# Attention and gated convolution FFN on one core: scores of three pairs in other PSUM banks, one load queue, a shared buffer pool, planned constants, and new due times

## The chip, the cores and the metric

The kernel runs on one core of one Trainium2 chip. The metric is the device time of one execution in microseconds; the median of 3 runs of the kernel before is 542.69 us (542.3 to 543.33). Lower is better. The five engines are called PE (TensorE, matmul; its weight loads are shown apart as PEld), DVE (VectorE), ACT (ScalarE), POOL (GpSimd) and SP (SyncE, which here only issues transfers).

## The reference

Eight batches of 576 rows. First a masked attention with 8 heads of 64: the first four heads see the last 32 positions, the other four see 32 positions at a distance of 4. Then a feed-forward block with a convolution of three taps along the rows as its gate.

```python
scores = (q @ k.T) / 8                       # per batch and head, 576 x 576
plain   = (rel >= 0) & (rel < 32)            # heads 0..3
dilated = (rel >= 0) & (rel < 128) & (rel % 4 == 0)   # heads 4..7
attn = softmax(where(mask, scores, -1e9));  x = attn @ v     # -> (8, 576, 512)
h = relu(x @ w_in)                           # 512 -> 1024
conv = sum(conv_w[k] * h shifted by k - 1)   # 3 taps along the rows
out = (h * sigmoid(conv)) @ w_out            # 1024 -> 512
```

## The kernel before, in words

**Pairs.** Each batch has four pairs of heads (`attention(b, p)`; p 0 and 1 plain, 2 and 3 dilated). Only the band that the mask lets through is computed. Per pair: SP loads `qk` and `v`; PE computes the scores into three of the four banks of the PSUM buffer `att` (`scores`, L255); the softmax runs on DVE and ACT; DVE transposes (L298); PE multiplies with `v` into the same `att` buffer (`values`, L309); ACT copies the high part of x (L359) and DVE subtracts to get the low part (L375). There is one `att` buffer, and a pair holds it once from its scores to its exponentials and once from its values to its subtraction. The first 8 pairs (those of batches 0 and 1) are "eased": PE adds the mask into the bank by matmuls with a matrix of ones (L244), DVE takes maxima (L265, L267), and ACT does nine exponentials of 64 columns with a bias and a running sum (L275). The other 24 pairs add the mask and sum on DVE (L280 to L292).

**Products.** `expert(b, ...)` multiplies x by `w_in` (L398, 16 groups of 12 matmuls a batch: three terms, high and low parts) in the PSUM buffers `mm` (two banks; in batch 0 also `nn`), ACT takes the relu into `h` (L405), ACT and DVE form the three taps (L416, L410), the sigmoid (L421), the gate (L423) and its high and low parts in `g` (L426, L428). The second product (L440, 36 blocks of 24 matmuls) accumulates in `nn` (two banks), ACT copies it to `out` (L451) and SP stores it (L454).

**Weights.** The weights come as 64-bit numbers. `weights` loads a 512 KB tile as pairs of 32-bit words into an `out` buffer, by a transfer issued from POOL (L466), and rebuilds it: one ACT pass (L473), then DVE steps (L475, L478, L480, L483, L486). For the first nine tiles (all eight of `w_in`, one of `w_out`) PE sums the parts (L495 to L497) and ACT copies high and low (L492, L500); for the other seven DVE adds and subtracts (L502, L508).

**Constants.** At the head, outside the plan, in this order on ACT: the mask is loaded by ACT's own queue and spread into `mask_sb` (L518 to L522), after that come the matrices `minus` and `ones` (L512, L513). In the program that runs, the first weight tile's ACT pass stands between the two.

**Order.** Nothing runs in loop order. Each piece of work is a `Task` with an engine, a cost and a due time; `Planner.order` simulates the engines and writes the order out: on each engine, of the tasks that could start within 0.25 us of the earliest, the one with the smallest due time goes next. Buffers are pools of slots; a task whose slot isn't free waits in that simulation. The due times are the tables `DUE` (products, gates, second products of each batch), `PAIR`, `WI` and `WO`. The chip executes each engine's and each queue's list strictly in that order, with semaphores where data or slots demand it.

Of the kernel before, what the change touches and what calls it, by code (L numbers as in the profile page):

```python
# [8 lines left out]
F32 = mybir.dt.float32  # L9
# [25 lines left out]
    0: (580.8, 27.9, -1.4),  # L35
    1: (213.6, -299.0, 236.5),
    2: (298.7, 74.3, 336.3),
    3: (207.5, 235.5, 370.3),
    4: (392.2, 246.5, 569.0),
    5: (236.9, 118.2, 411.6),  # L40
    6: (240.1, 311.5, 692.5),
    7: (425.8, 381.5, 859.4),
}
PAIR = {
    0: (-457.5, -556.4, -489.6, -298.9),
    1: (-233.9, -88.4, -68.9, 30.4),
    2: (100.4, 158.5, 106.2, 115.4),
    3: (159.5, 176.7, 263.5, 224.6),
    4: (271.0, 337.4, 174.1, 173.0),
    5: (406.9, 395.3, 384.0, 446.3),  # L50
    6: (231.2, 489.6, 330.6, 394.1),
    7: (590.7, 577.9, 625.9, 591.3),
}
WI = (-419.2, 32.4, -71.8, -195.1, -259.0, 8.1, -51.2, -117.3)
WO = (47.2, 77.7, 55.2, 78.0, 38.6, 19.0, 87.9, 102.0)
AHEAD = (8.0, 4.1, 0.0)
ONE = dict(start=True, stop=True, skip_group_check=True)


class Buffer:  # L60


    def __init__(self, pool):
        self.pool, self.left, self.end, self.t = pool, 0, 0.0, None
# [10 lines left out]
class Planner:  # L75

    LATENCY = {"DVE": 0.05, "ACT": 0.05, "SP": 2.0, "POOL": 3.0, "E": 0.2, "S": 0.33, "T": 0.35, "V": 0.2}
    OVERLAP = {"DVE": 0.08, "ACT": 0.095}
    GAP = 0.035
    WINDOW = 0.25  # L80
# [17 lines left out]
    def start(self, t, last, mode):  # L98
        at = 0.0
        if last is not None:  # L100
            at = last.end + (0.0 if t.engine == "PE" else self.GAP if last in t.after else -self.OVERLAP.get(t.engine, 0.0))
        for p in t.after:
            if p.engine != t.engine or p.engine == "SP":
                at = max(at, p.end + self.late(p))
        for b in t.uses:
            if b.t is None:
                if not self.free[b.pool]:
                    return None
                at = max(at, min(self.free[b.pool])[0])
# [49 lines left out]
def attn_moe(ctx: ExitStack, tc: tile.TileContext, qk_p, qk_d, v_p, v_d, w_in, w_out, conv, mask, out):  # L159
# [26 lines left out]
    slots("x", 7, [128, S], F32R, 2)  # L186
# [37 lines left out]
    xs = {}  # L224

    def attention(b, p):
# [3 lines left out]
        sc, tv = Buffer("att"), Buffer("att")  # L230
        xs[b, p] = x
        eased = NP * b + p < EASED
        n = (S + KP, QD + KD)[kind]
        lq = plan.add("SP", n * 0.0017, due - AHEAD[0], lambda: nc.sync.dma_start(
            out=qk.t[:, :n], in_=(qk_p, qk_d)[kind][b, p % 2]), uses=[qk])
        lv = plan.add("SP", 1.35, due - AHEAD[1], lambda: nc.sync.dma_start(
            out=v.t, in_=(v_p, v_d)[kind][b, p % 2]), uses=[v])

        def scores():


            if eased:
                for bank, (c0, c1) in enumerate(((0, 256), (320, 576), (256, 320))):
                    nc.tensor.matmul(sc.t[:, bank, 0:c1 - c0], ones, mask_sb[:, kind, c0:c1], start=True, stop=True,  # L244
                                     skip_group_check=True)
# [3 lines left out]
            for n in order:  # L249
                for hd in range(2):  # L250
# [3 lines left out]
                    for i, (q, k) in enumerate(parts):  # L254
                        nc.tensor.matmul(sc.t[quad * 32:quad * 32 + 32, bank, c * W:c * W + W], q, k,  # L255
                                         start=i == 0 and not eased, stop=i == len(parts) - 1, skip_group_check=True)

        last = plan.add("PE", (0.8, 0.92)[kind] + (0.5 if eased else 0.0), due, scores, [lq], [qk, sc, s], "S")
# [3 lines left out]
        banks = lambda: sc.t[:, 0:2, 0:256].rearrange("p h (a k) -> p h a k", k=W)  # L262
        if eased:

            last = plan.add("DVE", 0.68, due + 1.5, lambda: nc.vector.tensor_reduce(  # L265
                out=m.t.rearrange("p (h a) -> p h a", h=2)[:, :, 0:4], in_=banks(), axis=AX.X, op=ALU.max), [last], [sc, m])
            last = plan.add("DVE", 0.215, due + 1.5, lambda: nc.vector.tensor_reduce(  # L267
                out=m.t[:, 4:5], in_=sc.t[:, 2, 0:W], axis=AX.X, op=ALU.max), [last], [sc, m])
# [3 lines left out]
            def exps():  # L272
                for i in range(9):
                    bank, c = (0, i) if i < 4 else (2, 0) if i == 4 else (1, i - 5)
                    nc.scalar.activation(out=s.t[:, i, :], in_=sc.t[:, bank, c * W:c * W + W], func=AF.Exp,  # L275
                                         scale=SCALE, bias=m.t[:, i:i + 1], accum_out=z.t[:, i:i + 1])

            last = plan.add("ACT", 2.2, due + 3.0, exps, [last], [sc, s, m, z], "exp")
        else:
            last = plan.add("DVE", 0.68, due + 1.5, lambda: nc.vector.tensor_tensor(  # L280
                out=heads(flat()), in0=banks(), in1=heads(mask_sb[:, kind]), op=ALU.add),
                [last], [sc, s])
            last = plan.add("DVE", 0.215, due + 1.5, lambda: nc.vector.tensor_tensor(
                out=s.t[:, 4], in0=sc.t[:, 2, 0:W], in1=mask_sb[:, kind, 4 * W:5 * W], op=ALU.add), [last], [sc, s])
# [16 lines left out]
        def values():  # L301
# [6 lines left out]
            def pv(quad, hd, bank, block, c0, o, n):  # L308
                nc.tensor.matmul(tv.t[hd * 64:hd * 64 + 64, bank, o:o + n],  # L309
# [52 lines left out]
        if b < HELPED:  # L362
            def less():
                main, rest = parts(x.t[0])
                for t in range(4):
                    n = 160 - t % 2 * 32 if kind == 0 else 128
# [249 lines left out]
```

## Time and profile before

| | |
|---|---|
| median of 3 runs | 542.69 us (542.3 to 543.33) |
| the profiled execution, own time | 542.24 us |
| its span, first to last instruction | 540.4 us |
| busy in the span: PE / DVE / ACT / POOL | 509.5 / 400.1 / 310.0 / 10.3 us |
| mean granted TensorE clock | 0.983 |
| HBM read, written | 41.66 MB, 9.44 MB |

The profile is of one execution. Times inside it count from the first instruction of the span. A view by stretches gives the busy time of each engine in a stretch; the chain of waits follows, from the last instruction backwards, what released each step; the groups give, for one line, engine and shape, the count, the busy time and the mean of one. Matmuls overlap each other, so that the mean of one is longer than the distance from one to the next; that distance is read from the chain, where a row with a count gives the time of so many in sequence.

### The profile page before, as it was taken

The page shows a single profiled execution, that of the slowest core. Times are in us where ns is not written, and L with a number is a line of the kernel's source. Part 1 is how long each engine was busy: PE and PEld are TensorE (multiplying, and loading weights), DVE is VectorE, ACT ScalarE, POOL GpSimd, SP SyncE. Part 2 cuts the span into 40 slices and gives each one's busy share as a digit, 9 for nine tenths or more (in the row PEclk, how much of TensorE's full clock was granted, in tenths as well). Part 3 has the DMA queues.
Part 4 walks back from the last instruction along what each step waited for, and adds up shares of the span by engine and source line. Part 5 has one row for each costly group of instructions (what it writes and reads, how often), then busy time and mean ns, then how long its engine had stood idle before and what let it go on. Part 6 is the DMA issues. An engine that isn't in the chain of part 4 may idle for free.

```text
span 540.4 us, 17510 instructions
## 1 busy us (share of the span) xinstructions
PE 509.5 (94%) x7836; PEld 442.1 (82%) x7836; DVE 400.1 (74%) x692; ACT 310.0 (57%) x662; POOL 10.3 (2%) x29
## 2 busy tenths in 40 slices
PE   1678997999999999999999999999999999999997
PEld 1446896897887799879988889879989988889985
DVE  0999999899999789986893479985869309847910
ACT  3766989653764266843773158735677318528710
POOL 1011000000000000000000000000000000000000
PEclk9889997899999999999999999999999999999999
DMA  7656533222226542152113331151102012100011
GB/s 279 222 188 244 162 119 113 90 78 84 70 78 200 187 153 101 32 149 97 52 50 99 115 117 46 32 188 54 52 30 71 21 40 70 41 22 21 0 40 58
DMA packets 17162, 52.21 MB, mean 97 GB/s; under 512 B 1968, under 2 KB 2368, under 8 KB 17088
## 3 DMA queue, kind: packets, MB, share of 16 engines
q1 hardware_dynamic: 14608, 42.61, 23.9%
q0 software_dynamic: 2336, 8.41, 4.6%
q8 instruction: 61, 1.00, 0.8%
q10 hardware_dynamic: 144, 0.08, 0.1%
q14 instruction: 13, 0.11, 0.1%
HBM read 41.66 MB, written 9.44 MB: 95 GB/s over the span
## 4 chain that ended last, share of the span: by engine, by line
PE 75%; DVE 13%; ACT 9%; DMA 1%; issue 1%; ACTq 0%; POOL 0%; POOLq 0%; DVEq 0%
PE nn L440 33%; PE mm L398 30%; PE att L309 6%; PE att L255 4%; ACT s L275 4%; DVE c L410 3%; DMA out<-in_w_in_dram 1%; DVE s L296 1%; DVE pt L298 1%; DVE c L423 1%; PE nn L495 1%; DVE m L265 1%; ACT c L421 1%; ACT c L416 1%; ACT L289 0%
## 5 line engine op out<-in xcount | busy, mean ns | idle before, releaser
L410 DVE SCALAR_TENSOR_TENSOR c<-h,conv_sb,c 128x576 f32<-128x576 f32 x128 | 103.4, 815 | 22.7 <-ACT c L416 21.0
L405 ACT ACTIVATE h<-mm 128x288 f32<-128x288 f32 x120 | 48.1, 410 | 52.3 <-PE mm L398 50.7
L451 ACT COPY out<-nn 128x512 f32<-128x512 f32 (+1 forms) x37 | 21.1, 572 | 64.5 <-PE nn L440 61.7
L309 PEld LDWEIGHTS att<-pt,v 32*64 32x64 f32 x2944 | 37.9, 135 | 17.6 <-ACT s L275 5.2
L423 DVE TENSOR_TENSOR c<-c,h 128x576 f32<-128x576 f32 x64 | 47.3, 753 | 6.2 <-ACT c L421 5.3
L416 ACT ACTIVATE c<-h,conv_sb 128x576 f32<-128x576 f32 x64 | 49.0, 777 | 1.5
L398 PE MATMUL mm<-x3a,wi 128*128 128x288 f32 x176 | 49.7, 297 | 0.0
L421 ACT ACTIVATE c<-c 128x576 f32<-128x576 f32 x64 | 42.5, 681 | 11.4 <-DVE c L410 10.7
L309 PE MATMUL att<-pt,v 32*64 32x64 f32 (+2 forms) x2944 | 41.4, 229 | 6.7 <-ACT s L275 3.4
L398 PE MATMUL mm<-x4a,wi 128*128 128x288 f32 x160 | 45.7, 300 | 0.1
L398 PE MATMUL mm<-x2a,wi 128*128 128x288 f32 x144 | 41.1, 300 | 0.0
L255 PEld LDWEIGHTS att<-qk 64*32 64x32 f32 x2432 | 29.5, 109 | 9.2 <-issue 4.0
L398 PE MATMUL mm<-x5a,wi 128*128 128x288 f32 x128 | 36.5, 300 | 0.0
L398 PE MATMUL mm<-x6a,wi 128*128 128x288 f32 x128 | 36.1, 297 | 0.0
L255 PE MATMUL att<-qk 64*32 64x64 f32 x2432 | 34.9, 232 | 0.7 <-DVE x2b L375 0.6
L398 PEld LDWEIGHTS mm<-x3a,wi 128*128 128x128 f32 x176 | 33.0, 188 | 0.4
L398 PE MATMUL mm<-x0a,wi 128*128 128x288 f32 x112 | 31.6, 298 | 0.0
L398 PE MATMUL mm<-x1a,wi 128*128 128x288 f32 x112 | 31.5, 296 | 0.0
L291 DVE TENSOR_REDUCE z<-s 128x9 f32<-128x576 f32 x24 | 17.9, 748 | 18.2 <-ACT s L289 18.1
L398 PEld LDWEIGHTS mm<-x4a,wi 128*128 128x128 f32 x160 | 30.2, 189 | 0.9 <-ACT h L405 0.5
L440 PE MATMUL nn<-wo,g5a 128*128 128x512 f32 x72 | 28.9, 402 | 0.0
L440 PE MATMUL nn<-wo,g4a 128*128 128x512 f32 x72 | 28.9, 402 | 0.0
(170 smaller groups left out, 1330.9 us busy)
## 6 DMA issues: line engine op xcount, KB each, us to landing
qk<-in_qk_d_dram SPq DMA_DIRECT2D x16, 664.0 KB, 4.0
qk<-in_qk_p_dram SPq DMA_DIRECT2D x16, 592.0 KB, 4.1
out_dram<-out SPq DMA_DIRECT2D x31, 256.0 KB, 2.0
v<-in_v_p_dram SPq DMA_DIRECT2D x16, 384.0 KB, 3.5
v<-in_v_d_dram SPq DMA_DIRECT2D x16, 384.0 KB, 3.4
out<-in_w_in_dram POOLq DMA_DIRECT2D x8, 512.0 KB, 5.0
out<-in_w_out_dram POOLq DMA_DIRECT2D x8, 512.0 KB, 3.6
out_dram<-out SPq DMA_DIRECT2D x10, 128.0 KB, 2.3
```

The lines of the kernel that those rows point to most:

```text
L255: nc.tensor.matmul(sc.t[quad * 32:quad * 32 + 32, bank, c * W:c * W + W], q, k, start=i == 0 and not eased, stop=i == len(parts) - 1, skip ...
L275: nc.scalar.activation(out=s.t[:, i, :], in_=sc.t[:, bank, c * W:c * W + W], func=AF.Exp, scale=SCALE, bias=m.t[:, i:i + 1], accum_out=z.t ...
L291: last = plan.add("DVE", 0.755, due + 3.5, lambda: nc.vector.tensor_reduce(out=nine(z.t), in_=nine(s.t), axis=AX.X, op=ALU.add), [last], [ ...
L309: nc.tensor.matmul(tv.t[hd * 64:hd * 64 + 64, bank, o:o + n], v.t[quad * 32:quad * 32 + 32, block // 2, block % 2 * 64:block % 2 * 64 + 64 ...
L398: nc.tensor.matmul(ps.t[:, 0:HALF], wi[jw][fc][:, k * 128:k * 128 + 128], x[k].t[jx][:, hf * HALF:hf * HALF + HALF], start=(k == 0 and i = ...
L405: relu.append(plan.add("ACT", 0.4, due + 1.6 * u + 1.6, lambda fc=fc, hf=hf, ps=ps: nc.scalar.activation(out=h[fc].t[:, 1 + hf * HALF:1 + ...
L410: nc.vector.scalar_tensor_tensor(out=c[fc].t, in0=h[fc].t[:, k:S + k], scalar=conv_sb[:, k, fc:fc + 1], in1=c[fc].t, op0=ALU.mult, op1=ALU ...
L416: t = plan.add("ACT", 0.777, d, lambda fc=fc: nc.scalar.activation(out=c[fc].t, in_=h[fc].t[:, 1:S + 1], func=AF.Copy, scale=conv_sb[:, 1, ...
L421: t = plan.add("ACT", 0.686, d + 1.0, lambda fc=fc: nc.scalar.activation(out=c[fc].t, in_=c[fc].t, func=AF.Sigmoid), [t], [c[fc]], "sigmoid")
L423: t = plan.add("DVE", 0.755, d + 1.5, lambda fc=fc: nc.vector.tensor_tensor(out=c[fc].t, in0=c[fc].t, in1=h[fc].t[:, 1:S + 1], op=ALU.mult ...
L440: nc.tensor.matmul(ps.t, g[k].t[jg][:, col:col + 128], wo[jw][k], start=(k == 0 and i == 0), stop=(k == NF - 1 and i == 2))
L451: t = plan.add("ACT", 0.16 + 0.00093 * (c1 - c0), out_due + 5.6 + 5.6 * u, lambda ps=ps, o=o, c0=c0, c1=c1: nc.scalar.copy(out=o.t[:, c0:c ...
```

## The change

- **Scores of pairs 2 to 4 (batch 0, p = 1, 2, 3; `EARLY`)** no longer use `att` but both `mm` banks and one `nn` bank. Batch 0's first products wait in the plan for these scores. All eight banks become one PSUM tile, `banks`, with the pools as lists of bank numbers.
- **Masks of the eased pairs** come straight from the loaded `kinds_sb`, spread by a repeating read, with 4 (plain) or 5 (dilated) matmuls instead of 3. The spreading of `mask_sb` on ACT, which the other 24 pairs need, becomes planned tasks with due time 70.
- **Constants planned.** The load of the mask goes first on SP; the identity, `ones` and `minus` are tasks with the earliest due times.
- **One queue.** The 16 weight tiles and the taps are loaded from SP instead of POOL, in one list with `qk`, `v` and the stores. They get four buffers of their own (`raw`) instead of sharing the three of `out`.
- **Shared pool.** `h`, `c` and `out` (three each) become ten `u` buffers of [128, 578]; a task that takes one for `h` must leave two free (`spare`). The taps' result now starts at word 1 of its buffer, the stored result at word 16. The two-part `w` buffers (two) become three single ones.
- **`SUMMED`**: 12 tiles instead of 9 are summed on PE: three more of `w_out`.
- **Planner**: other costs (loads, exponentials), a wait of 2.3 us behind SP tasks, first times per engine; **all due times are new**. A branch that was switched off (`HELPED = 0`) is gone.

The core of the diff:

```diff
 DUE = {
-    0: (580.8, 27.9, -1.4),
-    1: (213.6, -299.0, 236.5),
...
-    7: (425.8, 381.5, 859.4),
+    0: (57.5, 90.4, 43.3),
+    1: (-112.3, 166.0, 223.7),
...
+    4: (-0.4, 293.4, 1016.3),
...
+    7: (-57.9, 355.7, 466.1),
 PAIR = {
-    0: (-457.5, -556.4, -489.6, -298.9),
-    1: (-233.9, -88.4, -68.9, 30.4),
+    0: (-155.8, -194.5, -384.9, -185.6),
+    1: (-9.5, -339.1, -101.5, 54.3),
...
-WI = (-419.2, 32.4, -71.8, -195.1, -259.0, 8.1, -51.2, -117.3)
-WO = (47.2, 77.7, 55.2, 78.0, 38.6, 19.0, 87.9, 102.0)
+WI = (-36.6, -51.1, -44.4, -350.5, -319.7, 42.1, -78.8, -407.0)
+WO = (109.7, 15.2, 69.3, 82.8, 128.6, 116.8, 106.8, 179.0)
+MASKS = 70.0
+EASED = range(8)
+EARLY = (1, 2, 3)
+SUMMED = range(12)
+LEFT = 16
+NU, NX, NR, NW, NT = 10, 7, 4, 3, 2
...
-    LATENCY = {"DVE": 0.05, "ACT": 0.05, "SP": 2.0, "POOL": 3.0, ...
+    LATENCY = {"DVE": 0.05, "ACT": 0.05, "SP": 2.3, "POOL": 0.1, ...
+    FIRST = {"SP": 0.75, "POOL": 1.0, "PE": 4.5, "ACT": 2.5}
...
-    hs = slots("h", 3, [128, S + 2])
-    slots("c", 3, [128, S])
-    slots("out", 3, [128, 1024])
-    slots("w", 2, [128, 512], F32, 2)
+    us = slots("u", NU, [128, S + 2])
+    slots("raw", NR, [128, 1024])
+    slots("w", NW, [128, 512])
...
+    banks = psum.tile([128, 8, 512], F32, name="banks")
+    plan.pool("att", [0])
+    plan.pool("mm", [4, 5])
+    plan.pool("nn", [6, 7])
...
-        sc, tv = Buffer("att"), Buffer("att")
+        early = NP * b + p in EARLY
+        sc, tv = [Buffer(n) for n in (("mm", "mm", "nn") if early else ("att",))], Buffer("att")
...
             if eased:
-                for bank, (c0, c1) in enumerate(((0, 256), (320, 576), (256, 320))):
-                    nc.tensor.matmul(sc.t[:, bank, 0:c1 - c0], ones, mask_sb[:, kind, c0:c1], ...)
+                own = ((0, 1), (2, 3)), ((2, 4),), ((1, 1),)
+                if kind == 1:
+                    own = ((3, 1), (2, 3)), ((3, 1), (2, 3)), ((4, 1),)
+                for bank, runs in enumerate(own):
+                    c = 0
+                    for i, n in runs:
+                        nc.tensor.matmul(banks[:, at[bank], c * W:(c + n) * W]..., ones,
+                                         kinds_sb[:, i, :].unsqueeze(1).to_broadcast([128, n, W]), ...)
...
-        last = plan.add("POOL", 2.2 * f, due - AHEAD[2], lambda: nc.gpsimd.dma_start(
+        last = plan.add("SP", 0.1 + 1.4 * f, due - AHEAD[2], lambda: nc.sync.dma_start(
...
-    nc.scalar.dma_start(out=kinds_sb, in_=mask)
-    make_identity(nc, ident)
-    nc.scalar.mul(out=minus, in_=ident, mul=-1.0)
-    nc.scalar.copy(out=ones, in_=ident)
+    kinds = plan.add("SP", 0.3, -1e4, lambda: nc.sync.dma_start(out=kinds_sb, in_=mask))
+    made = plan.add("POOL", 0.6, -1e4, lambda: make_identity(nc, ident))
+    made = plan.add("ACT", 0.29, -1e4, lambda: nc.scalar.copy(out=ones, in_=ident), [made])
+    plan.add("ACT", 0.29, -1e4, lambda: nc.scalar.mul(out=minus, in_=ident, mul=-1.0), [made])
...
+        masked[kind] = plan.add("ACT", 0.72, MASKS, lambda k=kind: nc.scalar.copy(out=slot_masks[k], in_=spread(2, 10)), [kinds])
```

More of the change, by code (lines that the diff above doesn't have):

```diff
@@ L98, in start @@
     def start(self, t, last, mode):
-        at = 0.0
+        at = self.FIRST.get(t.engine, 0.0)
         if last is not None:
@@ L104, in start @@
                 at = max(at, p.end + self.late(p))
+        wanted = {}
         for b in t.uses:
             if b.t is None:
-                if not self.free[b.pool]:
-                    return None
-                at = max(at, min(self.free[b.pool])[0])
+                wanted[b.pool] = wanted.get(b.pool, b.spare) + 1
+        for pool, n in wanted.items():
+            free = self.free[pool]
+            if len(free) < n:
+                return None
+            at = max(at, min(free)[0] if n == 1 else sorted(free)[n - 1][0])
         if t.table is not None and mode is not None and t.table != mode:
@@ L361, in attention @@
             his.append(last)
[L362 to L366, printed above, removed]
-                    nc.tensor.matmul(tv.t[:, t, 0:n], minus, main[:, t] if kind else (main, rest)[t % 2][:, t // 2],
-                                     start=False, stop=True, skip_group_check=True)
-                for g in range(2 if kind == 1 else 0):
-                    nc.tensor.matmul(src(1)[:, g], minus, rest[:, g], start=False, stop=True, skip_group_check=True)
-            last = plan.add("PE", (0.42, 0.6)[kind], due + 7.2, less, his, [tv, x], "E")
-            return [plan.add("ACT", cost, due + 7.5, lambda i=i: nc.scalar.copy(out=dst(x.t[1], i), in_=val(i)),
-                             [last], [tv, x]) for i, cost in ((0, 0.6), (1, 0.21))]
         return [plan.add("DVE", cost, due + 7.5, lambda i=i: nc.vector.tensor_tensor(
@@ L491, in weights @@
             ps = Buffer("nn")
[L492 removed]
+            part = plan.add("ACT", 0.62, due, lambda: nc.scalar.copy(out=hi, in_=words(t)), [main], [t])
             def add():
[L495 to L500 removed]
+                nc.tensor.matmul(bank(ps), ident, words(t), start=True, stop=False)
+                nc.tensor.matmul(bank(ps), minus, r.t, start=False, stop=False)
+                nc.tensor.matmul(bank(ps), minus, hi, start=False, stop=True)
+            last = plan.add("PE", 1.43, due, add, [rest, part], [t, r, ps], "E")
+            return plan.add("ACT", 0.6, due, lambda: nc.scalar.copy(out=lo, in_=bank(ps)), [last], [ps])
         last = rest
[L502 to L503 removed]
+        last = step(0.53, [t, r], lambda: nc.vector.tensor_tensor(
+            out=words(t) if dst is None else dst, in0=words(t), in1=words(r), op=ALU.add))
         if dst is not None:
@@ L506, in weights @@
         hi, lo = pair
-        last = plan.add("ACT", 0.62, due, lambda: nc.scalar.copy(out=hi, in_=t()), [last], [w])
-        return step(0.53, [w], lambda: nc.vector.tensor_tensor(out=lo, in0=t(), in1=hi.bitcast(F32), op=ALU.subtract))
-    nc.scalar.dma_start(out=kinds_sb, in_=mask)
-    make_identity(nc, ident)
-    nc.scalar.mul(out=minus, in_=ident, mul=-1.0)
-    nc.scalar.copy(out=ones, in_=ident)
+        last = plan.add("ACT", 0.62, due, lambda: nc.scalar.copy(out=hi, in_=words(t)), [last], [t])
@@ L523, in attn_moe @@
-    for h, in hs:
-        nc.gpsimd.memset(h[:, 0:1], 0.0)
-        nc.gpsimd.memset(h[:, S + 1:S + 2], 0.0)
-    wired = [weights(w_in[c], 512, WI[c], pair=(wi[0][c], wi[1][c]), summed=c < SUMMED) for c in range(NF)]
+    masked = [None, None]
+    for kind, (rest, own) in enumerate(((0, lambda: nc.scalar.copy(out=slot_masks[0][:, 0:5:4, :], in_=kinds_sb[:, 0:2, :])),
+                                        (1, lambda: nc.scalar.copy(out=slot_masks[1][:, 0:6:5, :], in_=spread(3, 2))))):
+        masked[kind] = plan.add("ACT", 0.72, MASKS, lambda k=kind: nc.scalar.copy(out=slot_masks[k], in_=spread(2, 10)), [kinds])
+        masked[kind] = plan.add("ACT", 0.29, MASKS, own, [masked[kind]])
@@ L527, in attn_moe @@
+    masked[1] = plan.add("ACT", 0.24, MASKS, lambda: nc.scalar.copy(out=slot_masks[1][:, 4, :], in_=kinds_sb[:, 4, :]),
+                         [masked[1]])
+    wired = [weights(w_in[c], 512, WI[c], pair=(wi[0][c], wi[1][c]), summed=c in SUMMED) for c in range(NF)]
     conved = weights(conv, 3 * NF, -4.0, dst=conv_sb.rearrange("p t c -> p (t c)"))
-    wored = [weights(w_out[c], 512, WO[c], pair=(wo[0][c], wo[1][c]), summed=c < SUMMED - NF) for c in range(NF)]
+    wored = [weights(w_out[c], 512, WO[c], pair=(wo[0][c], wo[1][c]), summed=c + NF in SUMMED) for c in range(NF)]
```

178 lines of the change are left out of this document (88 added, 90 removed).

## The prediction

> **What bounds the kernel now.** I read the page first, then the busy time by stretches, then the chain of waits of the first 50 us, then the groups and waits behind its steps.
>
> ```profile
> span 540.4 us, 17510 instructions
> PE 509.5 (94%) x7836; PEld 442.1 (82%) x7836; DVE 400.1 (74%) x692; ACT 310.0 (57%) x662; POOL 10.3 (2%) x29
> ...
> 0.00:12.40 12.40, 1.96 (x75) 1.41 (x75) 0.01 (x1) 4.22 (x9) 2.59 (x15) 1.00 0.79 301
> 12.40:46.00 33.60, 23.14 (x633) 14.08 (x633) 30.47 (x71) 23.03 (x97) 3.18 (x6) 0.90 0.61 200
> 46.00:100.00 54.00, 48.76 (x983) 43.17 (x979) 49.86 (x95) 44.11 (x136) 3.38 (x6) 0.91 0.49 161
> 100.00:240.00 140.00, 139.14 (x2400) 119.80 (x2399) 128.16 (x223) 80.92 (x143) 1.16 (x2) 1.00 0.33 105
> 240.00:520.00 280.00, 279.98 (x3682) 250.30 (x3681) 191.56 (x304) 155.34 (x274) 0.00 (x0) 1.00 0.19 62
> ```
>
> The columns of a stretch are its length, then PE, PEld, DVE, ACT and POOL busy with their counts, the granted clock, the DMA share and GB/s. From 100 us on PE is the bound: busy for 139.1 of 140 and 280.0 of 280 us. Ahead of that it idles 10.4 + 10.5 + 5.2 = 26.1 us, and its clock there is 0.9. In that head the full engine is DVE: nothing in the first 12.4 us, then 30.5 of 33.6, then 49.9 of 54.0. So the end follows from when PE's full stretch begins, and that follows from DVE's head. Whatever moves the head forward by S takes S off the end, as long as work added to PE finds room in the 26 idle microseconds. The chain tells why the head starts late (start, length, what):
>
> ```profile
> 1.44 7.83 DMA out<-in_w_in_dram
> ...
> 10.15 0.20 ACT ones L513
> ...
> 11.05 1.31 PE att L255 x70
> 12.39 0.69 DVE m L265
> ...
> 13.52 2.78 ACT s L275 x18
> ...
> 22.50 1.15 PE att L309 x66
> ...
> 26.30 1.61 PE att L309 x79
> ...
> 28.66 0.82 DVE x1b L375 x2
> 29.48 0.34 DVE w1a L475
> 29.85 0.44 DVE w1b L478
> 30.31 0.70 DVE w1b L480
> 31.04 0.44 DVE w1a L483
> 31.50 0.69 DVE r L486
> ...
> 33.23 2.78 ACT s L275 x18
> ...
> 39.09 2.78 ACT s L275 x18
> ...
> 44.72 1.36 PE att L309 x81
> 46.09 2.18 PE mm L398 x15
> ```
>
> Two things stand out. First, `ones` waits on ACT behind the first weight tile, a 512 KB transfer that takes until 9.27 us; the first scores wait for `ones`, and DVE for the scores. Second, the third pair's exponentials (33.23) come some 14 us after the second's: `att` is held by the two values (22.50, 26.30) until the subtraction at 28.66 ends, then DVE runs a weight tile's five steps (29.48 to 32.19) ahead of the maxima. The first product starts at 46.09. By 100 us, 210 products are done:
>
> ```profile
> 0.00:100.00 100.00, 31.97 (x210) 0.91 0.57 191
> ...
> 407.39 19.27 PE mm L398 x144
> 509.30 27.22 PE nn L440 x120
> ```
>
> The first row is L398 alone; one batch is 16 x 12 = 192 products, so at 100 us batch 0 is through and batch 1 just begun. The chain's rows give the full rate, 19.27/144 = 0.134 us: a batch of products is 25.7 us of PE.
>
> **The change part by part.**
>
> *Start: `ones`, masks, loads.* `ones` no longer stands behind a weight tile, and the 80 KB of masks no longer have to be spread first. What ends last is then the first pair's load. By due time less 8.0 (for `qk`), the SP list begins: masks, `w_in` tile 7, `qk` and `v` of batch 0 p = 2, tile 3, `qk` and `v` of batch 1 p = 1, tile 4. The scores need 80 + 512 + 664 KB, 1.29 MB. Rates and waits:
>
> ```profile
> 2.00:4.00 2.00, 0.00 (x0) 0.00 (x0) 0.00 (x0) 0.46 (x1) 1.41 (x4) 1.00 0.81 283
> 4.00:6.00 2.00, 0.00 (x0) 0.00 (x0) 0.00 (x0) 0.51 (x1) 0.00 (x0) 1.00 1.02 414
> ...
> POOL out L466 <- DVE z L293: 27.2, 4, 13.2
> ...
> SPq L234 <- PE att L255: 48.6, 9, 12.9
> ```
>
> 0.57 MB by 4 us and the other 0.72 at 0.414 MB/us give 5.7 us; I add 1 us for the end of a transfer (an estimate: tile 7 of old, 1.44 to 9.27, carries that too). Scores at 6.7, ended after 2 us (from `ones`, 10.35, to 12.36 before, mask matmuls included) at 8.7 instead of 12.4: 3.7 us earlier. Tile 7 itself is there at about 4.7, so DVE does its five steps (2.7 us, 29.48 to 32.19) before the first maxima. DVE's work starts at 5.5 instead of 12.4. Bounds: 0 (if the queue's data come no earlier than before) and 6.9.
>
> The Trainium skill, DMA: Bandwidth & Descriptors, section "Issuing engines are not separate DMA queues", says that transfers from several engines share the same 16 DMA engines and that issuing from more of them saves only issue time. The trace agrees in so far as SP's and POOL's first transfers together run into 414 GB/s with a DMA share of 1.02. By the rule one queue in place of two brings nothing and costs nothing but issue; my sum takes nothing for it either, only the order within the queue.
>
> *Pairs 2 to 4 in `mm` and `nn`.* Scores no longer wait for another pair's values. What is late next is the bank pair of `mm`: an early pair's scores wait until the previous one's exponentials end. The cadence is scores and masks (2.0, or 1.3 warm), maxima (0.69 and then to the exponentials' start, 12.39 to 13.52 = 1.1), exponentials 2.78: about 5.5 us, and a pair through `att` fits between. From 8.7: exponentials of the three early pairs start at 9.8, 15.5 and 21, those of batch 0's remaining pair (p = 0, through `att`) by 27 and end by 29.8; then normalising, transpose, values and split, which the last pair of old took from 41.87 (39.09 + 2.78) to 46.09, that is 4.2. First product at about 34 by this chain. DVE's own sum is the other limit: with batch 1's p = 1 in between, five pairs and four tiles. In 12.4 to 46.0 DVE did four pairs and what is left of 30.47 us in tiles, all that the products waited for; the new list is about as long, so 5.5 + 30.5 = 36.0. I take 36, the later of the two: the first product comes 10 us earlier. Bounds: 3.7 (only the start counts, the cadence is DVE's) and 12.
>
> *Twelve tiles summed on PE.* DVE loses two steps for each of three tiles:
>
> ```profile
> L502 DVE TENSOR_TENSOR w0b<-w0b,w0a 128x512 f32<-128x512 f32 x5 | 3.4, 689 | 0.1
> L508 DVE TENSOR_TENSOR wo<-w0b,wo 128x512 fp32r<-128x512 f32 x5 | 3.4, 686 | 0.0
> ...
> 49.53 1.12 PE L495 MATMUL nn<-w1b,ident 128*128 128x512 f32 x2
> ...
> 50.95 0.29 PE L398 MATMUL mm<-x3a,wi 128*128 128x288 f32 x1
> ```
>
> 3 x (0.689 + 0.686) = 4.1 us less on DVE, most of it inside DVE's full stretch: I take 3. PE gets three sums of 50.95 - 49.53 = 1.42, 4.3 us. ACT gets three copies instead of DVE, in a stretch where it has 9.9 of 54 us free. PE also gets 12 more mask matmuls for 8 pairs; three take 0.41 at most in the row below, so they cost under 1.6. PE's 5.9 us lie in the head, where 26 us are idle; uncovered they cost all 5.9. I take 2, since `w_out` tiles 1 to 3 (due 15 to 83) come when PE is already filling.
>
> ```profile
> 48.29 0.41 PE L244 MATMUL att<-mask_sb,ones 128*128 128x256 bf16 x3
> ...
> L410 DVE SCALAR_TENSOR_TENSOR c<-h,conv_sb,c 128x576 f32<-128x576 f32 x128 | 103.4, 815 | 22.7 <-ACT c L416 21.0
> ```
>
> *Shared pool.* Eight `h` can be filled before any is gated, where there were three. One gated column block costs DVE two taps of 0.815 and two more steps, about as much as PE's 25.7/8 = 3.2 us for its products; so with three buffers the products of batch 0 ran in step with DVE, which at the same time owed tiles and pairs. Now they can run ahead. I take 0 on top of S: DVE's total is unchanged, and what is run ahead is waited for later. Bounds: -2 to +4. Starting the taps' result at word 1 costs 0: L410 reads `h` at words 0 and 2 in one group of one mean, 815 ns.
>
> *One queue.* The 17 loads on SP cost issue, and a head that waits now holds up every load and store behind it. Before, SP waited 48.6 us for `qk` slots by 120 us while POOL's loads went past it. The plan knows of the list; I take 0, bounds 0 to 16 lost (rival 2).
>
> *New due times.* From 100 us on PE idles 0.9 us by busy time until 240 and nothing until 520; there is little to win and some to lose there. I take 0, bounds -3 to +4.
>
> Sum: 10 + 3 - 2 = 11 us. The profiled execution's own time is 542.24 (span 540.4); 542.24 - 11 = 531.2. The median of the runs is 0.45 above that execution, so I say 531.
>
> **The rivals.**
>
> *1. Only DVE's own gain arrives.* The earlier products are waited for again, because gates, tiles and the second batch's pairs are the same DVE work and DVE was 92% busy from 46 to 100. Then S is 3.7 + 3 - 2 = 4.7 us, 537. For it: those 49.9 of 54 us. Against: DVE itself starts 6.9 us earlier, with tile 7.
>
> *2. Slower: the single SP queue blocks.* Its place is 15 to 120 us, where tile loads wait for `raw` slots and `qk` loads for scores. POOL's waits on slots were up to 13.2 us, 27.2 in four; SP's on scores up to 12.9. In one list such a wait delays pairs, and a late pair leaves DVE without work. It decides from 11 us of delay that nothing covers; one wait of 12.9 ahead of a pair's load, plus the 5.7 us worked out above until a load behind others has landed, is 18.6, so 7.6 more than the gain: 550. Against: the tiles get four slots instead of sharing three with stores, and the first four need no wait at all.
>
> *3. Nothing measurable.* The head's gain is lost in the 100 to 240 us stretch, where DVE is already at 128.2 of 140 us and new due times move its work: 542.
>
> *4. The clock comes back too.* In the head the granted clock is 0.90 to 0.91 for 87.6 us, so some 8 us of full clock are missing; if the denser pairs leave shorter gaps, part comes back where PE is the limit. With half of it 531 - 4 = 527. The Trainium skill, TensorE: Matmul & The Clock Gate, section "HAM oscillation", says that idle gaps over about 3.4 us put the clock back to half. The trace agrees that the loss lies only where PE idles: 1.00 from 100 us on.
>
> **How the numbers follow.** Chances: forecast 0.50 (own range 526 to 536), rival 1 0.15, rival 2 0.17, rival 3 0.05, rival 4 0.13. Faster is forecast, 1 and 4: 0.78; same 0.05; slower 0.17. About 0.2%, 1.1 us, is what a measurement of this kernel can tell from no change. The likeliest is 531. The range runs from 521 (the upper ends together: 12 for the pairs, 4.1 for the tiles at no cost to PE, 4 for the pool, and a little of the clock) to 545 (all of rivals 1 and 3, and the near part of 2).
>
> **What would show it.** Right: first exponentials near 10 us instead of 13.52; three score groups in the head without values between them; first product near 36; over 250 products (210 + 11/0.134 = 292 at the full rate, some of it taken by sums) by 100 us; DVE busy from about 6 us; PE full from about 90. Wrong: a `qk` load on SP that waits over 10 us behind a tile's slot; a first product later than 42; DVE under 85% busy in 46 to 100; or PE below 97% busy between 100 and 510 us.

## The result, and the profile after

The changed kernel takes 530.14 us (median of 4 runs, 529.47 to 531.54) against 542.98 us of the kernel before (542.3 to 543.33) on the same chip: a ratio of 0.977 (95%: 0.974 to 0.979), 12.8 us. The forecast was 531. The profiled execution took 529.47 us. Its page and its stretches (columns as in the prediction):

```profile
span 527.7 us, 17587 instructions
PE 509.0 (96%) x7860; PEld 442.6 (84%) x7860; DVE 399.0 (76%) x686; ACT 304.7 (58%) x659; POOL 1.4 (0%) x26
```

```profile
0.00:12.40 12.40, 6.16 (x167) 4.17 (x167) 6.03 (x13) 8.23 (x29) 1.37 (x26) 1.00 0.84 319
12.40:46.00 33.60, 25.50 (x804) 16.87 (x803) 30.83 (x76) 25.58 (x105) 0.00 (x0) 0.85 0.76 263
46.00:100.00 54.00, 53.69 (x760) 49.48 (x760) 52.02 (x96) 47.40 (x131) 0.00 (x0) 1.00 0.38 124
100.00:240.00 140.00, 139.85 (x2385) 120.56 (x2384) 118.76 (x203) 73.78 (x130) 0.00 (x0) 1.00 0.32 103
0.00:100.00 100.00, 85.35 (x1727) 70.53 (x1728) 88.89 (x183) 81.20 (x262) 1.37 (x26) 0.95 0.56 195
```

PE's whole busy time stays (509.0 against 509.5 us) although it got three more sums and more mask matmuls (at most 5.9 us by the prediction's rows); what the span lost is idle time. By 100 us PE idled 6.2 + 8.1 + 0.3 = 14.6 us instead of 26.1, after that 0.2 instead of 0.9 until 240. From 46 us on PE is full and its clock is 1.00, where it was 0.91 until 100 before. DVE worked 88.9 us by 100 instead of 0.0 + 30.5 + 49.9 = 80.3, and owed 4.1 less: it is 12.7 us further, as much as the span gained (540.4 - 527.7 = 12.7).

The chain of waits of the head, in the order of time:

```profile
2.58 6.51 DMA raw<-in_w_in_dram
...
15.57 2.78 ACT s L302 x18
...
18.39 1.96 PE banks L336 x80
20.35 2.00 PE banks L507 x2
22.36 0.43 PE banks L508
22.78 0.43 PE banks L509
23.21 1.29 PE banks L336 x70
...
32.44 1.38 ACT s L302 x8
...
33.86 1.59 PE banks L336 x63
35.46 1.97 PE banks L507 x2
...
37.90 1.31 PE banks L336 x81
...
43.59 0.83 DVE x4b L389 x2
...
44.47 0.30 PE banks L265 x3
44.77 1.06 PE banks L278 x66
45.83 4.16 PE banks L413 x30
```

The chain no longer starts on `ones` but on the load of the second weight tile, and goes through all of DMA, ACT, DVE and PE. The first product starts at 45.83 us, as before (46.09). But a fifth pair (`x4b`) is split by then, and the scores of a sixth are done (L278 at 44.77); before, three pairs were split and the fourth's values had just ended. Exponentials in the first 46 us (nine a pair; count, shortest, median and longest ns, first and last start), here of after:

```profile
L302 ACT ACTIVATE s<-banks,m x45: 303/332/412, 9.8 to 33.3; 128x64 f32<-128x64 f32 x45
```

and of before:

```profile
L275 ACT ACTIVATE s<-att,m x36: 305/326/352, 13.5 to 41.4; 128x64 f32<-128x64 f32 x36
```

Five pairs' exponentials have begun by 33.3 us, where four took until 41.4. The weight tiles that DVE has worked on by 46 us (the form with 24 columns is the taps), of after and then of before:

```profile
L493 DVE SCALAR_TENSOR_TENSOR w<-raw,w x8: 184/693/693, 6.9 to 44.7; 128x512 int32<-128x512 int32 x7, 128x24 int32<-128x24 int32 x1
```

```profile
L480 DVE SCALAR_TENSOR_TENSOR w0b<-out,w0b x4: 184/692/693, 14.2 to 45.0; 128x512 int32<-128x512 int32 x3, 128x24 int32<-128x24 int32 x1
L480 DVE SCALAR_TENSOR_TENSOR w1b<-out,w1b x3: 693/693/693, 20.4 to 39.8; 128x512 int32<-128x512 int32 x3
```

That is seven tiles instead of six. The products by 100 us are 299 instead of 210:

```profile
0.00:100.00 100.00, 41.27 (x299) 0.95 0.56 195
```

At 0.134 us each (the prediction's row of the full rate) the 89 are 11.9 us. The waits until 46 us, and two of the SP queue's over the whole span (waiter, releaser: total us, times, longest):

```profile
PE banks L336 <- ACT s L302: 6.3, 4, 3.4
DVE w L489 <- ACT w L487: 5.9, 1, 5.9
...
PE banks L278 <- DMA qk<-in_qk_d_dram: 3.6, 1, 3.6
```

```profile
SPq L481 <- DVE w L498: 15.1, 2, 13.7
SPq L481 <- DVE r L498: 13.9, 6, 4.7
```

SP does wait in front of a weight tile's load (L481) for a `raw` buffer, once for 13.7 us (from 66.6 to 80.3 us), and PE is full all the same.

Which pairs these are shows in the names: batch 0's products read `x0`, `x2`, `x3` and `x4`, so the second pair, `x1`, is batch 1's first one, which goes through `att`. The exponentials start at 9.78 (batch 0's p = 2, early), 15.57 (batch 1's p = 1, through `att`), 21.12 (p = 1, early), 28.38 (p = 3, early) and 31.0 (p = 0, through `att`). The last pair's end at 33.82, and until then `att` is held by its scores. The values of p = 1, whose transposed exponentials are ready by 26.8, wait for it: PE idles 3.4 us until 32.38, does four matmuls, and goes on from 33.86; those of p = 3 (37.90) and of p = 0 (40.84) follow one after the other through the same `att`. From the end of the exponentials to the first product it takes 12.0 us.

### The profile page after: what moved, and what is told of

Same layout as the page of the kernel before. It is cut to its first block, busy times and chain, and to the rows that moved or that the text cites. A ratio compares the mean times of both kernels' runs of the same rounds, so it can differ in the third digit from the quotient of the medians.

```text
span 527.7 us, 17587 instructions
## 1 busy us (share of the span) xinstructions
PE 509.0 (96%) x7860; PEld 442.6 (84%) x7860; DVE 399.0 (76%) x686; ACT 304.7 (58%) x659; POOL 1.4 (0%) x26
## 4 chain that ended last, share of the span: by engine, by line
PE 93%; DVE 2%; ACT 2%; DMA 1%; issue 0%; SPq 0%; ACTq 0%
PE banks L455 39%; PE banks L413 39%; PE banks L336 7%; PE banks L278 5%; PE banks L507 2%; ACT s L302 2%; DMA raw<-in_w_in_dram 1%; PE banks L508 0%; PE banks L509 0%; DVE pt L325 0%; DVE w L493 0%; DVE r L498 0%; DVE m L291 0%; DVE w L491 0%; PE banks L265 0%
## 5 line engine op out<-in xcount | busy, mean ns | idle before, releaser
L425 DVE SCALAR_TENSOR_TENSOR u<-u,conv_sb,u 128x576 f32<-128x576 f32 x128 | 103.7, 817 | 40.2 <-ACT u L431 38.5
L420 ACT ACTIVATE u<-banks 128x288 f32<-128x288 f32 x128 | 50.8, 412 | 55.9 <-PE banks L413 55.4
L438 DVE TENSOR_TENSOR u<-u,u 128x576 f32<-128x576 f32 x64 | 47.8, 758 | 19.8 <-ACT u L436 19.0
L336 PEld LDWEIGHTS banks<-pt,v 32*64 32x64 f32 x2944 | 39.1, 136 | 17.8 <-ACT s L302 7.2
L436 ACT ACTIVATE u<-u 128x576 f32<-128x576 f32 x64 | 42.7, 682 | 17.7 <-DVE u L425 17.4
L431 ACT ACTIVATE u<-u,conv_sb 128x576 f32<-128x576 f32 x64 | 49.6, 776 | 1.2
L336 PE MATMUL banks<-pt,v 32*64 32x64 f32 (+2 forms) x2944 | 43.2, 230 | 6.9 <-ACT s L302 6.3
L413 PE MATMUL banks<-x4a,wi 128*128 128x288 f32 x160 | 45.0, 296 | 0.0
L413 PE MATMUL banks<-x0a,wi 128*128 128x288 f32 x160 | 44.9, 296 | 0.0
L413 PE MATMUL banks<-x6a,wi 128*128 128x288 f32 x160 | 44.8, 295 | 0.0
L413 PE MATMUL banks<-x1a,wi 128*128 128x288 f32 x160 | 44.7, 294 | 0.0
L278 PEld LDWEIGHTS banks<-qk 64*32 64x32 f32 x2432 | 29.0, 107 | 13.9 <-issue 4.9
L278 PE MATMUL banks<-qk 64*32 64x64 f32 x2432 | 34.4, 227 | 4.6 <-DMA qk<-in_qk_d_dram 3.6
L413 PE MATMUL banks<-x2a,wi 128*128 128x288 f32 x128 | 35.9, 295 | 0.0
L413 PE MATMUL banks<-x5a,wi 128*128 128x288 f32 x128 | 35.8, 295 | 0.0
L413 PE MATMUL banks<-x3a,wi 128*128 128x288 f32 x128 | 35.8, 294 | 0.0
L413 PEld LDWEIGHTS banks<-x6a,wi 128*128 128x128 f32 x160 | 30.0, 188 | 0.4
L413 PEld LDWEIGHTS banks<-x4a,wi 128*128 128x128 f32 x160 | 30.0, 188 | 0.2
L413 PEld LDWEIGHTS banks<-x0a,wi 128*128 128x128 f32 x160 | 30.0, 188 | 0.1
L413 PEld LDWEIGHTS banks<-x1a,wi 128*128 128x128 f32 x160 | 30.0, 188 | 0.1
L455 PE MATMUL banks<-wo,g4a 128*128 128x512 f32 x72 | 29.2, 406 | 0.0
```

The source lines that it names most:

```text
L278: nc.tensor.matmul(banks[quad * 32:quad * 32 + 32, at[bank], c * W:c * W + W], q, k, start=i == 0 and not eased, stop=i == len(parts) - 1, ...
L336: nc.tensor.matmul(banks[hd * 64:hd * 64 + 64, bank, o:o + n], v.t[quad * 32:quad * 32 + 32, block // 2, block % 2 * 64:block % 2 * 64 + 6 ...
L413: nc.tensor.matmul(bank(ps)[:, 0:HALF], wi[jw][fc][:, k * 128:k * 128 + 128], x[k].t[jx][:, hf * HALF:hf * HALF + HALF], start=(k == 0 and ...
L420: relu.append(plan.add("ACT", 0.4, due + 1.6 * u + 1.6, lambda fc=fc, hf=hf, ps=ps: nc.scalar.activation(out=h[fc].t[:, 1 + hf * HALF:1 + ...
L425: nc.vector.scalar_tensor_tensor(out=body(c[fc]), in0=h[fc].t[:, k:S + k], scalar=conv_sb[:, k, fc:fc + 1], in1=body(c[fc]), op0=ALU.mult, ...
L431: t = plan.add("ACT", 0.777, d, lambda fc=fc: nc.scalar.activation(out=body(c[fc]), in_=body(h[fc]), func=AF.Copy, scale=conv_sb[:, 1, fc: ...
```

## The experiments

Two theories were set against each other. One: DVE's list sets when PE becomes full, and every microsecond of the 12.7 is DVE's. The other: the head is one chain through loads, ACT, DVE and PE, and the gain comes from its order, so that work on any engine costs part of its length. Times are compared with the runs of the kernel before that were made on the same chip (542.55, 543.77 and 543.21 us in three groups), so the last column, the time gained over those, is what to compare; the change has 12.8. "PE idle" and "products" are those of the profiled execution's first 100 us; for e3 that execution was its slowest (535.3 us).

| kernel | median us | ratio (95%) | PE idle | products | gain, us |
|---|---|---|---|---|---|
| e1_dve_more | 533.72 | 0.983 (0.981 to 0.984) | 16.4 | 272 | 8.8 |
| e2_act_more | 532.14 | 0.980 (0.978 to 0.982) | 14.0 | 289 | 10.4 |
| e3_pe_more | 532.12 | 0.981 (0.977 to 0.984) | 11.4 | 264 | 10.4 |
| e4_no_early | 543.57 | 1.000 (0.998 to 1.002) | 21.4 | 207 | -1.0 |
| e5_head | 538.14 | 0.990 (0.986 to 0.993) | 22.2 | 224 | 5.6 |
| e6_head_due | 535.19 | 0.986 (0.983 to 0.989) | 21.6 | 240 | 8.6 |
| e7_split | 538.27 | 0.990 (0.988 to 0.992) | 20.0 | 192 | 5.5 |
| e8_pool_queue | 537.62 | 0.989 (0.987 to 0.991) | 20.1 | 198 | 6.2 |
| e9_sum9 | 543.43 | 1.000 (0.998 to 1.002) | 26.0 | 192 | -0.2 |
| e10_banks_only | 543.69 | 1.000 (0.998 to 1.002) | 24.2 | 192 | -0.5 |
| e11_early_023 | 528.69 | 0.973 (0.970 to 0.976) | 12.7 | 312 | 14.5 |
| e12_w4_raw3 | 530.57 | 0.976 (0.972 to 0.980) | 14.3 | 305 | 12.6 |

Of the ranges that were expected before each run, e5 and e11 fell into one; e3 and e7 missed one by less than 0.3 us; the other eight fell into none (e4, e8, e9 and e10 were slower than any that had been expected).

**Added work on one engine.** Three kernels with the order of the changed one, in which one step of each of the nine tiles due before 50 us is done twice.

```diff
 # e1: the third DVE step (L493)
-        last = step(0.53, [raw, u, t], lambda: nc.vector.scalar_tensor_tensor(...))
+        last = step(0.53, [raw, u, t], lambda: [nc.vector.scalar_tensor_tensor(...)
+            for _ in range(2 if summed and due < 50.0 else 1)])
 # e2: the copy of the high part on ACT (L504)
-            part = plan.add("ACT", 0.62, due, lambda: nc.scalar.copy(out=hi, in_=words(t)), [main], [t])
+            part = plan.add("ACT", 0.62, due, lambda: [nc.scalar.copy(out=hi, in_=words(t)) for _ in range(2 if due < 50.0 else 1)], [main], [t])
 # e3: PE's first matmul of a sum (L507)
+                if due < 50.0:
+                    nc.tensor.matmul(bank(ps), ident, words(t), start=True, stop=True)
```

> The changed kernel with one DVE step (L493, 0.69 us) issued twice in the nine summed tiles that come first (all of w_in, one of w_out), 6.2 us of DVE work more in the head; order, results and everything else unchanged. Theory A (the end follows DVE's work in the head: it started 6.5 us earlier, idles 2 us less from 46 to 100 us and has 4.1 us less to do): the end moves by nearly all of it, 530.1 + 5 to 6 = 535 to 536. Rival B (what gained is that PE runs ahead of DVE, through the other banks and the ten buffers, so that DVE has slack): 530 to 532. Rival C (the order of the new due times at large, no single engine): 530 to 533.

> The changed kernel with ACT's copy of the high part (L504, 0.62 us) issued twice in the same nine tiles, some 5 us of ACT work more in the head; the rest unchanged. Theory A: ACT has slack (47.4 of 54 us busy from 46 to 100), so 530 to 531.5. If ACT, with its nine exponentials a pair, is what paces the head instead of DVE: 534 to 535.

> The changed kernel with the first matmul of the sum (L507, two passes, 0.5 us at full clock and up to 1 in the head) issued twice in the same nine tiles, 4.5 to 7 us of PE work more; the rest unchanged. Theory A: seven of the nine lie before 46 us, where PE idles 14 us, two behind it: 531 to 532. If PE's own work already sets the head: 535 to 537.

The doubled step of e1 by form in the first 50 us, its stretch until 100 us and its products (L413) there, and PE's busy time in e3:

```profile
L493 DVE SCALAR_TENSOR_TENSOR w<-raw,w 128x512 int32<-128x512 int32 x15 | 10.4, 692 | 0.5
```

```profile
0.00:100.00 100.00, 83.62 (x1700) 67.67 (x1701) 91.04 (x187) 77.85 (x257) 1.37 (x26) 0.93 0.57 195
```

```profile
0.00:100.00 100.00, 37.68 (x272) 0.93 0.57 195
```

```profile
PE 517.8 (97%) x7878; PEld 446.2 (84%) x7878; DVE 399.2 (75%) x686; ACT 304.4 (57%) x659; POOL 1.4 (0%) x26
```

Nine times 0.692 is 6.2 us on DVE; it cost 3.6 us by the medians, 4.0 by the gains, about 0.6 of the dose (the work added), and the first product came 2.6 us later (48.4). By 100 us 27 products are missing, 27 x 0.134 = 3.6 us. Nine copies of ACT (about 0.64 each, 5.8 us) cost 2.0 to 2.4 us, about 0.4 of the dose. Nine more matmuls of sums cost the same by the medians; they had been estimated at 4.5 to 7 us, but PE was busy for 517.8 us instead of 509.0, so the dose was some 8.8 us and the share about a quarter. That profiled execution itself took 5.8 us longer than the change's, so PE's share is the least certain. The intervals of e2 and e3 overlap the change's; that of e1 does not. So what is shown is that 6.2 us more on DVE cost less than 6.2 us, against the first theory, which wanted the whole dose; that ACT and PE have a part too is likely, not shown.

**Without the early scores.** The changed kernel, same due times, where no pair uses the banks of the products.

```diff
-EARLY = (1, 2, 3)
+EARLY = ()
```

> The changed kernel with EARLY empty: scores of pairs 2 to 4 in att again, planned anew with the same due times. Theory A: DVE fills the wait with tiles, so the loss is what it can't fill: 531 to 535. Rival B (the banks are what gained): most of the 10 us that the prediction gave them comes back, 538 to 541.

Its chain shows what comes back:

```profile
15.51 2.68 ACT s L302 x18
...
18.23 1.96 PE banks L336 x79
20.20 2.00 PE banks L507 x2
...
23.05 1.55 PE banks L336 x70
...
30.27 2.78 ACT s L302 x17
...
59.28 1.60 PE banks L336 x65
...
65.61 2.17 PE banks L413 x15
```

The second pair's exponentials are early (15.51), but the third pair's start at 30.27 (28.4 is the changed kernel's fourth): two values (L336) and a sum stand between, as `att` is held. The first product comes at 65.61, and the whole gain is gone. With this order of work the early banks carry all of it; but these due times were made for them, so 13 us is not their price alone.

**The head alone.** The kernel before with planned constants and the masks straight from `kinds_sb`, everything else and the due times as before (e5); then with the new planner costs and with due times searched anew (e6). Here and below, "searched" means that the tables were varied until the plan's own simulated end came no earlier.

```diff
-    nc.scalar.dma_start(out=kinds_sb, in_=mask)
-    make_identity(nc, ident)
-    nc.scalar.copy(out=ones, in_=ident)
+    kinds = plan.add("SP", 0.3, -1e4, lambda: nc.sync.dma_start(out=kinds_sb, in_=mask))
+    made = plan.add("POOL", 0.6, -1e4, lambda: make_identity(nc, ident))
+    made = plan.add("ACT", 0.29, -1e4, lambda: nc.scalar.copy(out=ones, in_=ident), [made])
```

> The kernel before with the head alone changed: masks' load first on SP, identity, ones and minus planned first, mask matmuls of the eased pairs straight from the loaded kinds, mask spreading later; att for all scores, POOL's load queue, three pools, nine sums and the due times of before. Theory A (DVE's head start is what gained): scores no longer wait for a weight tile, DVE starts some 3 to 5 us earlier, the end follows: 538 to 540. Theory B (the free banks gained: with them empty the changed kernel fell back to 543.6): the third pair still waits for two values in att, 541 to 543.

> The same old structure and new head (att for all scores, POOL's queue, three pools, nine sums), but with the new planner's costs and with due times searched anew for it in the plan's own simulation. Rival C (due times and a truer plan gained, not the parts): 531 to 534. Theory B (the banks): 537 to 541, since att still serialises scores and values.

The chain of e5:

```profile
1.60 6.82 DMA out<-in_w_in_dram
...
9.02 2.77 ACT s L282 x18
...
28.11 2.78 ACT s L282 x18
```

The first exponentials move from 13.52 to 9.02 us, the third pair's from 33.23 to 28.11; the time falls by 5.6 us (by the interval, 3.8 to 7.4). The new costs and due times on the same structure bring 3.0 more by the medians; the two intervals overlap (e5's runs go from 536.02 to 541.13 us, e6's from 534.94 to 537.42), so these 3.0 are not shown. If they hold, 8.6 of the 12.8 us are to be had with the old buffers, the old queues and nine sums, and the rest of the change has 4.2 us together: banks, queue, buffers and sums, and a small step that no run tests alone, ACT's copy of the high part (L504), which waits for DVE's third step on a tile instead of the fourth.

**Separate pools; weights from POOL.** The changed kernel with `h`, `c` and `out` in pools of their own (three, three and four buffers), and the changed kernel with the tiles and taps issued from POOL; each with due times searched anew.

```diff
 # e7
-    us = slots("u", NU, [128, S + 2])
+    us = slots("u", 3, [128, S + 2]) + slots("c", 3, [128, S + 2]) + slots("out", 4, [128, S + 2])
 # e8
-        last = plan.add("SP", 0.1 + 1.4 * f, due - AHEAD[2], lambda: nc.sync.dma_start(
+        last = plan.add("POOL", 2.2 * f, due - AHEAD[2], lambda: nc.gpsimd.dma_start(
```

> The changed kernel with the shared pool undone: three h, three c, four out buffers; due times searched anew for it. If running eight h ahead of the gates is part of the gain: 534 to 538. If the pool is worth nothing on top (the prediction's 0): 530 to 532.

> The changed kernel with the weight tiles loaded from POOL again (plan's cost and wait of before), due times searched anew. If one queue costs nothing and brings nothing but the order of the first loads: the first tile shares the transfer engines with the pairs' loads again, DVE starts 1 to 3 us later, 531 to 533. If the single queue was a burden that the rest covered: under 530.

Both lose about 7 us against the change (7.3 and 6.7 by the gains); e8 also takes back the plan's wait of 3.0 us behind POOL. In e8's chain the third pair waits for its load:

```profile
8.85 2.77 ACT s L302 x18
...
12.08 1.54 PE banks L278 x78
...
13.64 6.50 DMA qk<-in_qk_d_dram
...
20.18 1.60 PE banks L278 x76
```

The load (13.64, 6.5 us) could only be issued when the second pair's scores (12.08) had freed a `qk` buffer, and these had waited for the first pair's exponentials (8.85 to 11.62) to free the banks. So the third pair's scores come at 20.18, and what the chain shows is another order, not the price of a second queue.

**Nine sums; the early banks alone.** The changed kernel with `SUMMED = range(9)` (e9), and the head of e6 with the early banks added (e10: separate pools, POOL's queue, nine sums), both with due times searched anew. By its edit e10 also keeps the change's four `raw`, three `w` and four `out` buffers, so it differs from e6 in more than the banks.

```diff
-SUMMED = range(12)
+SUMMED = range(9)
```

> The changed kernel with nine tiles summed on PE as before, instead of twelve, and due times searched anew for it. DVE gets the 4.1 us of three tiles back, PE loses 4.3 us of sums, ACT three copies. If DVE's share of the head sets the end, as 6.2 us of added DVE work cost 3.6, this costs about 0.58 x 4.1 = 2.4 us or more: 532.5 to 536. If PE's total is what counts, it gains: 526 to 529.

> The head of e6_head_due plus the scores of pairs 2 to 4 in the banks of the products, and nothing else of the change: h, taps and results in pools of their own, weights loaded from POOL, nine sums; due times searched anew. If the banks are worth most of the gain by themselves, this comes to 533 or less, against 535.2 without the banks. If the banks need the shared pool and the single queue (scores done early only help when h and tiles can follow), it stays at 535 to 538.

Both theories missed for e9, which takes as long as the kernel before. The stretches of e9:

```profile
46.00:100.00 54.00, 46.87 (x660) 41.19 (x656) 47.21 (x90) 37.86 (x88) 0.00 (x0) 0.86 0.33 108
...
0.00:100.00 100.00, 74.04 (x1439) 59.20 (x1440) 83.48 (x172) 69.76 (x227) 1.37 (x26) 0.88 0.53 183
```

DVE got 4.1 us more work and did 5.4 us less of it by 100 us than in the changed kernel (83.5 against 88.9), ACT 11 us less. No engine is full (PE 46.9, DVE 47.2 of 54 us), so the loss isn't the price of three sums on DVE; it is an order with waits in it, the best that the search found. The same holds for e10 (DVE 79.95 us by 100), which is 9 us worse than e6, a kernel without early banks and with fewer buffers. What these two show is that in the order found for e10 the early banks bring nothing, and that a part can't be priced by taking it out here: the likely reason is that the search for due times doesn't come back to an equally good order. For the same reason the 7 us of e7 and e8 are not prices of the pool and the queue.

**Other choices of the same kind.** Pairs p = 0, 2, 3 early instead of 1, 2, 3 (e11), and the same with three `raw` and four `w` buffers (e12); due times searched on from those of the change.

```diff
-EARLY = (1, 2, 3)
+EARLY = (0, 2, 3)
 # e12 also
-NU, NX, NR, NW, NT = 10, 7, 4, 3, 2
+NU, NX, NR, NW, NT = 10, 7, 3, 4, 2
```

> The changed kernel with another choice of early pairs: p = 0, 2 and 3 of batch 0 use the product banks, and p = 1 goes through att; due times searched on from those of the change. If the number of pairs scored ahead of the values is what matters, not which, it gives 528.5 to 531, the same as the change within its noise. If the choice p = 1, 2, 3 matters (the kind of mask, the order of loads), 532 or more.

> As e11_early_023, but with three buffers for loaded weight tiles and four for the parts being rebuilt, instead of four and three; due times searched on. If the wait of a tile's load for its buffer is harmless, and DVE's tile steps wait for PE's sums, it gives 527.5 to 530; if the fourth load buffer is needed to keep the single queue moving, 531 to 535.

The stretches of e11 and of e12:

```profile
12.40:46.00 33.60, 28.60 (x808) 19.09 (x807) 31.47 (x72) 25.42 (x111) 0.00 (x0) 0.85 0.80 279
...
0.00:100.00 100.00, 87.29 (x1740) 71.70 (x1740) 89.83 (x184) 79.54 (x261) 1.37 (x26) 0.95 0.56 194
```

```profile
12.40:46.00 33.60, 28.33 (x728) 18.23 (x723) 29.18 (x66) 23.46 (x99) 0.00 (x0) 1.00 0.69 237
46.00:100.00 54.00, 53.55 (x852) 49.79 (x851) 51.66 (x102) 47.20 (x133) 0.00 (x0) 1.00 0.40 134
```

e11 has 312 products by 100 us, 13 more than the change, and a median 1.45 us lower (1.7 by the gains); its interval overlaps that of the change, so it is not shown to be better. Which pairs are early matters little, where the due times are searched on for it. e12 is not shown to differ from either: with a fourth `w` buffer in its place the fourth `raw` buffer isn't needed, in keeping with SP's harmless wait for one.

## Why the prediction came out right, and where its steps did not

**The bound: right.** All kernels with PE idle by 100 us of 20 us or more end at 535 us or later; the five at 530 to 534 have 11 to 16.4, and e11 12.7. After 100 us PE is full in every one (138.8 to 140 of 140 us until 240, 279 to 280 of 280 until 520). Within the slow group idle time does not rank the kernels: e4 (21.4) and e6 (21.6) end 8 us apart, with PE busy for 516.5 and 507.7 us; e4 has three more sums and a granted clock of 0.75 from 12.4 to 46 us, e6 0.90. Products by 100 us, at 0.134 us each, give the change's 11.9 of 12.7 us and e1's 3.6 of 3.6 to 4.0, but they fail from e5 to e8: e7 has 18 fewer than the kernel before and ends 5.5 us earlier, with 21 products of the second kind (L455) done by then where the kernel before had none.

**The start (scores at 8.7, DVE from 5.5): right.** DVE begins at 5.9, right behind the tile and ACT's pass (the wait of 5.9 us above); the scores run from 6.88 to 8.5 and the first exponentials start at 9.78. e5 prices a start like it by itself: 5.6 us, where 3.7 had been put to the scores; the third pair moved by 5.1 us.

**The cadence (9.8, 15.5, 21): right in the times, not in the pairs.** The trace of after has 9.78, 15.57 and 21.12 us, one pair every 5.5 to 5.8 us, and with the same due times but no early banks (e4) the third comes at 30.27. But the times had been worked out for the three early pairs; the second place went to batch 1's pair through `att`. The early pairs start at 9.78, 21.12 and 28.38, and p = 0, expected by 27, at 31.0.

**The first product at 36: wrong, and the 10 us in the sum hang on it.** It starts at 45.83. Both limits failed. DVE's was "the new list is about as long", five pairs and four tiles: ahead of the first product DVE did 6.03 + 30.83 = 36.9 us of work and not 30.5, with five pairs, seven tiles and the taps. The chain's was 4.2 us from the last exponentials to the first product: it took 12.0, because the values of three pairs went through the one `att` in turn and had waited for p = 0's scores to leave it. The early banks took the scores out of that queue and not the values. The fifth pair and the seventh tile were owed in 46 to 100 us in the old order, where PE then waited; PE's idle time there fell from 5.2 to 0.3 us and its products by 100 us came to 299 (292 in the prediction). Its own mark for being wrong, a first product later than 42, did not mean a lost gain.

**The total: partly luck.** The 10 us came not as an earlier first product but as work done ahead of it: by 100 us DVE is 8.6 us further than before, and 4.1 us less is owed, where the sum had 10 + 3 - 2. That 530.14 lies within 1 us of 531 also needs the parts put at nothing to have come to nothing in sum, which no run shows. And the sum's last step was rounded down: 542.24 - 11 + 0.45 is 531.7.

**Twelve sums (+3 for DVE, -2 for PE): consistent, not shown.** From the doses, 0.6 x 4.1 = 2.4 us for DVE, and for PE a quarter of at most 5.9 us, some 1.5 (an estimate from e3, whose share is uncertain). The net is near the +1 of the sum. The undoing (e9) could not size it.

**Shared pool 0 and one queue 0: not settled.** Taken out, they cost up to 7.3 and 6.7 us, far outside the bound of the pool (-2 to +4), but with another order. The Trainium skill, DMA: Bandwidth & Descriptors, section "Issuing engines are not separate DMA queues", leads one to expect nothing from the queue but issue time. e8 agrees as to the rate: from 8 to 10 us, with a DMA share of 1.00 in both, its two queues move 410 GB/s and the change's one queue 410. Its loss has not been shown to be the queue's.

**Due times 0: no reason for it in the head.** The stretch from 100 us on had been taken for all that they could touch; on the old structure new costs and due times gave 3.0 us by the medians (e6 against e5), and e9 and e10, which take as long as the kernel before, suggest that the order in the head decides 10 us and more.

**Rivals.** 1 (only DVE's gain, 537) fell: PE is full from 46 us, so the work done ahead is not waited for again. 2 (SP's queue blocks): its wait is there, 13.7 us, but falls where nothing waits for a load (PE is busy for 10.0 of 10 us from 70 to 80), and the next `qk` load is issued only at 118.8. (POOL's longest wait for a slot before was 19.3 us, on L486, and not 13.2.) 3 (the gain lost again until 240 us) fell: PE idles 0.2 us there, and DVE has 118.8 us of work instead of 128.2. 4 (the clock) is not settled. In 46 to 100 us, where PE is the limit, it rose from 0.91 to 1.00; in 12.4 to 46 it fell from 0.90 to 0.85. Busy time times missing clock gives 2.3 + 4.4 = 6.7 us before and 3.8 after, so 2.9 us of the gain can be the clock's (an estimate), and PE's busy time did stay the same with more work. Against it, e12, with 1.00 in both, takes 530.57 us, and its execution with the highest mean clock (0.999) is its slowest. For it, executions of one kernel with a lower mean clock tend to be longer: e5 took 536.02 and 536.54 us at 0.987, and 541.13 at 0.974. Which of the two follows from the other is not shown.

**Open** is how the 4.2 us between e6 and the change are shared among banks, pool, queue and sums: the banks, added to e6 with some buffers, show no gain (e10), and taken out, each costs more than all together have (e4, e7, e8, e9).

## What to carry to other kernels

Where one engine is full from some point to the end, count its idle time ahead of that point, not when its first instruction of a kind runs: the order decides that, and it may well put more preparation first. Work of one kind done by a fixed time (here products by 100 us) measures the same only between like orders. Where a resource is relieved for one use (here `att` of the scores), look for its next use in the same chain (the values). Where the order is searched, the parts of a change are hard to price by taking each out; add a known dose of work to each engine in the unchanged order instead, measure the dose in the trace, and expect shares (here 0.6 for DVE; for ACT and PE within the noise). Look first at what stands outside the plan: planning the constants was worth 5.6 of the 12.8 us.

## What the runs showed of the hardware that had not been expected

A tile's sum on PE takes up to 2.00 + 0.43 + 0.43 = 2.86 us in the head (at 20.35 us), twice the 1.42 that the prediction had from the row at 49.53 us; three such stand on the chain of e4, and the kernel before has one of 1.80 + 0.43 + 0.43 at 23.65. The granted clock there is 0.55 (20 to 24 us of after), and 0.60 in the kernel before (24 to 28). And the granted clock differs between profiled executions of like orders: 0.85 from 12.4 to 46 us in the change and in e11 with 25.5 and 28.6 us busy, 1.00 in e12 with 28.3. The Trainium skill, TensorE: Matmul & The Clock Gate, section "HAM oscillation", ties the loss to idle gaps of more than about 3.4 us; the clock is 1.00 here wherever PE has no gaps, and in after it falls to 0.50 at 34 us behind a gap of 3.4 us (28.96 to 32.38). But it is 0.50 from 17 to 23 us too, where no gap since 6.88 us was longer than 1.0 us, so neither the longest gap nor the busy time of a stretch alone tells.
